# Last chunk of a fused attention-and-GELU kernel: the two token pairs one after the other, and one pair's stores on two queues

## The chip, the cores and the metric

The kernel runs on one core of one Trainium2 chip. The metric is device time in microseconds (us) of one execution, from repeated executions; the profile is one further execution, taken by the hardware profiler. Five engines work side by side, each on its own instruction stream in order: TensorE (PE, with its weight loads shown as PEld), VectorE (DVE), ScalarE (ACT), GpSimd (POOL) and SyncE (SP). ACT and SP also issue transfers (DMAs); such an issue stands in the same stream as the engine's other instructions, and 16 DMA engines then move the data.

## What is computed

The reference, cut to its core (8 batches, 8 heads, sequence 576, head size 64; d_model 512, d_ff 2048):

```python
q_s = softmax(q, axis=-1);  k_s = softmax(k, axis=2)
kv  = einsum('bhsd,bhse->bhde', k_s, v)
att = einsum('bhsd,bhde->bhse', q_s, kv)
x   = att.transpose(0, 2, 1, 3).reshape(B * S, H * D)     # 4608 x 512
h   = x @ w_in                                            # 4608 x 2048
g   = 0.5 * h * (1.0 + erf(h / sqrt(2)))
out = g @ w_out                                           # 4608 x 512
```

All inputs and the output are float32. The kernel multiplies in bf16 and accumulates in float32.

## The kernel before, in words

Tokens are taken in nine chunks of 512: chunks 0 to 7 are the first 512 tokens of each batch, chunk 8 is the eight remainders of 64 tokens. Each chunk has an attention part (`kv_mm`, `x_mm`), a first matrix product with GELU (`h_phase`, `h_pairs` or `h_waves`), and a second matrix product. The order of all instructions is written out by hand: each engine runs its instructions in the order in which the program calls them, and the framework adds only the semaphore waits.

From chunk 1 on, the second product uses a seven-product scheme: the 512 tokens x 512 columns of output are four quadrants c11, c12 (tokens of the first half) and c21, c22 (second half), and instead of eight block products there are seven, `mm(1)` to `mm(7)`, whose left sides are blocks of `g` and sums of them (`s12`, `s5`, made on DVE by `s_parts`) and whose right sides are blocks of `w_out` and sums of them (`w16`, `w7`). Products that are accumulated in the same PSUM bank, and adds on DVE, put the quadrants together.

The last chunk has its own routine, `y_last` (L741 to L811), because nothing follows it that could hide its end. It splits each quadrant once more, into two halves of 128 token columns, j = 0 and j = 1 (the "token pairs"). For each j:

- Each `mm(j, m, ps, first)` (L763) is 8 matmuls of 256 columns into a PSUM bank `ps`; with `first` False it adds to what is in the bank. Product 7 of j = 1 is cut into two of 128 columns in two banks (L807).
- Product 4 goes to bank bd, and ACT copies it to `f`, a part of `zeros32` (L778). Product 5 goes to be, and DVE subtracts it from `f` (L783). Product 1 goes to ba, and DVE adds it to `f` for c22 (j = 0) or c11 (j = 1) (L785). Product 2 is accumulated on bd, and ACT copies the sum to c21 (L789). Product 3 goes to a bank bx (j = 0, copied by ACT at L781) or is accumulated on be (j = 1, copied by ACT at L794), for c12. DVE then completes c22 (L791, L796).
- Product 6 goes to bb and DVE adds it to c22 (L801). Product 7 of j = 0 is accumulated on ba, and DVE writes c11 = `f` + ba (L805); for j = 1 it goes to fresh banks and is added to c11 (L810).
- A quadrant's half is 128 partitions x 256 columns in SBUF, in the tiles `ysb` (`y_sb` in the profile). `store` (L753) sends it out in two DMAs of 64 partitions each (64 KB), u = 0 and u = 1, on the queues that it is given: `sp` is SP's, `act_q` is ACT's.

Before, there are two loops over j. The first makes products 4, (3,) 5, 1, 2 of j = 0 and then 4, 5, 1, 2, 3 of j = 1; the second makes 6 and 7 of j = 0, then 6 and 7 of j = 1. Every DVE add is recorded on the line of the helper `tt`, L428; every matmul of `y_last` on L765; every store on L755. In all there are 16 stores, 11 on SP and 5 on ACT.

Of the kernel before, what the change touches and what calls it, by code (L numbers as in the profile page):

```python
# [16 lines left out]
def kernel(  # L17
# [48 lines left out]
    def bank(i, name="ps", shape=(128, 512)):  # L66
        return psum.tile(list(shape), FP32, tag=f"k{i}", name=name)
# [359 lines left out]
    def tt(out, in0, in1, op=ALU.add, eng=nc.vector):  # L427
        eng.tensor_tensor(out=out, in0=in0, in1=in1, op=op)  # L428
# [232 lines left out]
    def y_operands(c):  # L661
        g = st[c]["g"]
        act = {
            1: s12[:, :, LO], 2: s12[:, :, HI], 3: g[:, UP, LO], 4: g[:, DN, HI],
            5: s5, 6: g[:, UP, HI], 7: g[:, DN, LO],
        }
        wgt = {
            1: w16[:, 0], 2: wo_bf[:, UP, 0:HN], 3: wo_bf[:, UP, HN:DM],
            4: wo_bf[:, DN, 0:HN], 5: wo_bf[:, DN, HN:DM], 6: w16[:, 1], 7: w7,
        }  # L670
        return act, wgt
# [69 lines left out]
    def y_last(c):  # L741

        act, wgt = y_operands(c)
        names = (("x0", "yd"), ("x2", "yx"), ("x1", "ye"), ("ba", "ya"), ("bb", "yb"),
                 ("x3", "yd"), ("kv0", "ye"), ("kv1", "yb"))
        bd, bx, be, ba, bb, bd1, be1, bb1 = (bank(roles[r], n) for r, n in names)
        banks = [(bd, be, bb, ba), (bd1, be1, bb1, None)]
        ysb = [moe_sb.tile([128, 2, DM], FP32, tag="y_sb", name="y_sb", bufs=2) for i in range(2)]  # L750
        dst = out.rearrange("(j u s) n -> u s j n", j=J, u=2)

        def store(half, j, c0, *engs):  # L753
            for u, eng in enumerate(engs):
                eng.dma_start(  # L755
                    out=dst[u, M:S, 2 * half + j, c0:c0 + HN],
                    in_=ysb[half][u * R:(u + 1) * R, j, c0:c0 + HN],
                )

        sp, act_q = nc.sync, nc.scalar  # L760
        halves = [[(bank(roles["x2"], "ya") if ps is None else ps)[:, 0:HN] for ps in banks[j]] for j in range(2)]

        def mm(j, m, ps, first, n=slice(0, HN)):  # L763
            for k in range(HK):
                nc.tensor.matmul(  # L765
                    ps[:, n], act[m][:, k, j * 128:(j + 1) * 128], wgt[m][:, k, n],
                    start=(first and k == 0), stop=(k == HK - 1), skip_group_check=True,
                )

        def parts(j):  # L770
            f = zeros32[:, j * HN:(j + 1) * HN]
            return (f, ysb[0][:, j, 0:HN], ysb[0][:, j, HN:DM], ysb[1][:, j, 0:HN], ysb[1][:, j, HN:DM])

        for j in range(2):
            bd, be, bb, ba = halves[j]
            f, c11, c12, c21, c22 = parts(j)
            mm(j, 4, bd, True)
            nc.scalar.copy(out=f, in_=bd)  # L778
            if j == 0:
                mm(j, 3, bx[:, 0:HN], True)  # L780
                nc.scalar.copy(out=c12, in_=bx[:, 0:HN])  # L781
            mm(j, 5, be, True)
            tt(f, f, be, ALU.subtract)  # L783
            mm(j, 1, ba, True)
            tt(c11 if j else c22, f, ba)  # L785
            if j == 0:
                tt(c12, c12, be)
            mm(j, 2, bd, False)
            nc.scalar.copy(out=c21, in_=bd)  # L789
            store(1, j, 0, sp, sp)  # L790
            tt(c22, c11 if j else c22, c21, ALU.subtract)  # L791
            if j:
                mm(j, 3, be, False)
                nc.scalar.copy(out=c12, in_=be)  # L794
            store(0, j, HN, act_q if j else sp, sp)
            tt(c22, c22, c12)  # L796
        for j in range(2):
            bd, be, bb, ba = halves[j]
            f, c11, c12, c21, c22 = parts(j)
            mm(j, 6, bb, True)  # L800
            tt(c22, c22, bb)  # L801
            store(1, j, HN, act_q, sp)
            if j == 0:
                mm(j, 7, ba, False)
                tt(c11, f, ba)  # L805
            else:
                for r, n in (("x0", slice(0, 128)), ("x1", slice(128, HN))):  # L807
                    ps = bank(roles[r], "ya")
                    mm(j, 7, ps, True, n)
                    tt(c11[:, n], c11[:, n], ps[:, n])  # L810
            store(0, j, 0, act_q, sp)  # L811
# [289 lines left out]
    for c in range(2, B + 1):  # L1101
        nb = c + 2
        if 2 < c and nb < B:
            load(nb)
        elif nb == B:
            load_qrest()
        h_waves(c, q_late if c == 2 else None)
        s_parts(c, 4, 4, (2,))
        yi = {}
        if nb <= B:  # L1110
            yi[8] = [lambda: exp_q(nb)]
            yi[1] = [lambda: norm_q(nb)]
            yi[3] = [lambda: table(AF.Gelu)]
        if nb < B:
            yi[9] = [lambda: exp_k(nb)]
            yi[0] = [lambda: touch_g(c), lambda: cast_v_all(nb)]
        if c < B:
            yi[5] = [lambda: next_x(c, nb)]
            y_phase(c, yi)
        else:  # L1120
            y_last(c)
# [30 lines left out]
```

## Time and profile before

| what | value |
|---|---|
| median of 3 runs | 256.82 us (256.74 to 257.05) |
| the profiled execution's own time | 257.07 us |
| its span | 255.3 us |
| granted TensorE clock over the span | 0.996 |
| PE busy in the last chunk's second product (238.7 to 251.2 us) | 12.42 of 12.50 us |
| last matmul of the program ends | 251.1 us |
| last DVE add | 251.16 to 251.45 us |
| last store: issue starts, issue takes, issue to landing | 252.20 us, 0.68 us, 2.1 us |
| bytes read from and written to HBM | 36.70 MB, 9.44 MB |

The span is what the profiler saw from the first to the last instruction; the execution's own time has 1.8 us around it. A line of a timeline has a start in us from the span's beginning, a duration in us, the engine, the source line, the operation, and out<-in; "x8" means that eight such instructions are merged into one line; in brackets, how long the engine had been idle and what released it. SPq and ACTq are the instruction queues of SP and ACT, on which DMA issues stand: the duration there is that of the issue, not of the transfer. "To landing" is the time from the start of an issue to the arrival of its last part.

### The profile page before, as it was taken

How to read it: one execution, taken by the hardware profiler on the slowest of the kernel's cores; microseconds unless marked ns; L12 is line 12 of the kernel's file. 1: busy time of each engine (PE TensorE's matmuls, PEld its weight loads, DVE VectorE, ACT ScalarE, POOL GpSimd, SP SyncE). 2: the span in 40 equal slices, each digit the busy share in tenths (PEclk: the TensorE clock that was granted, in tenths of full speed). 3: DMA queues.
4: the chain of work that ended last, by engine and by line, in shares of the span. 5: the costliest groups of instructions: out<-in, count | busy, mean ns of one | idle time of the engine just before them, and what ended most of it. 6: DMA issues, size and time to landing. Idle time of an engine off the chain costs nothing.

```text
span 255.3 us, 6533 instructions
## 1 busy us (share of the span) xinstructions
PE 248.8 (97%) x2678; PEld 196.1 (77%) x2678; DVE 208.1 (82%) x365; ACT 188.9 (74%) x320; POOL 67.8 (27%) x65
## 2 busy tenths in 40 slices
PE   7999999999999999999999999999999999999993
PEld 3444445448888888888888888888888888888882
DVE  1878796998986989897889788988898889488962
ACT  4875996699977995899589968896886787148720
POOL 1430034000735067006700580058001800040000
PEclk9999999999999999999999999999999999999998
DMA  7999999994449925980499059904920340022024
GB/s 236 396 389 424 403 406 399 400 410 166 62 143 335 265 65 126 328 336 1 114 299 369 7 95 314 374 3 86 270 63 3 82 164 3 0 87 82 1 54 113
DMA packets 43166, 50.23 MB, mean 197 GB/s; under 512 B 20224, under 2 KB 30464, under 8 KB 42880
## 3 DMA queue, kind: packets, MB, share of 16 engines
q1 hardware_dynamic: 42496, 49.19, 58.0%
q10 hardware_dynamic: 640, 0.62, 1.0%
q8 instruction: 21, 0.34, 0.5%
q14 instruction: 9, 0.07, 0.1%
HBM read 36.70 MB, written 9.44 MB: 181 GB/s over the span
## 4 chain that ended last, share of the span: by engine, by line
PE 93%; DMA 4%; POOL 1%; DVE 0%; issue 0%; SPq 0%
PE qa L497 19%; PE ps L377 11%; PE ya L694 10%; PE qb L497 10%; PE yd L694 10%; PE ye L694 6%; PE ps L637 5%; PE yb L694 5%; PE qc L497 5%; PE yx L694 4%; DMA f<-in_v_dram 2%; PE kv L225 2%; PE ps L343 2%; DMA f<-in_q_dram 2%; PE ya L765 1%; PE yd L765 1%
## 5 line engine op out<-in xcount | busy, mean ns | idle before, releaser
L497 PEld LDWEIGHTS <-quad_s 128*128 128x128 bf16 x448 | 43.8, 98 | 5.3 <-issue 0.2
L694 PEld LDWEIGHTS <-g 128*128 128x128 bf16 x448 | 43.3, 98 | 5.8 <-issue 0.4
L269 POOL TENSOR_TENSOR e<-e,recq 128x2048 bf16<-128x2048 bf16 (+1 forms) x9 | 27.4, 3048 | 72.5 <-DVE recq L264 47.4
L694 PEld LDWEIGHTS <-s 128*128 128x128 bf16 x336 | 32.9, 98 | 3.8
L497 PEld LDWEIGHTS <-wi_bf 128*128 128x128 bf16 x336 | 32.8, 98 | 3.9
L497 PE MATMUL qa<-quad_t,quad_s 128*128 128x256 bf16 x224 | 29.3, 272 | 0.0
L377 PE MATMUL ps<-xT,wi_bf 128*128 128x512 bf16 x128 | 28.1, 379 | 0.0
L428 POOL TENSOR_TENSOR y_sb<-y_sb 128x512 f32<-128x512 f32 x14 | 19.5, 1391 | 24.2 <-DVE y_sb L428 21.3
L263 DVE TENSOR_REDUCE qsum<-e 128x16 f32<-128x1024 bf16 (+1 forms) x12 | 20.9, 1742 | 5.0 <-ACT e L173 5.0
L377 PEld LDWEIGHTS <-wi_bf 128*128 128x128 bf16 x128 | 12.3, 97 | 15.2 <-issue 0.8
L428 DVE TENSOR_TENSOR qb<-qa,r 128x512 f32<-128x512 f32 x28 | 18.1, 693 | 5.8 <-ACT g L521 3.1
L505 ACT COPY qc<-qa 128x512 f32<-128x512 f32 x26 | 13.9, 577 | 12.0 <-PE qa L497 11.5
L383 ACT ACTIVATE g<-ps 128x512 bf16<-128x512 f32 x32 | 17.7, 602 | 6.0 <-PE ps L377 5.7
L521 ACT ACTIVATE g<-r 128x512 bf16<-128x512 f32 x28 | 17.3, 633 | 6.2 <-DVE r L428 6.2
L173 ACT ACTIVATE e<-f 128x512 bf16<-128x512 f32 (+1 forms) x42 | 20.5, 559 | 1.5 <-DMA f<-in_q_dram 1.4
L521 ACT ACTIVATE g<-qc 128x512 bf16<-128x512 f32 x28 | 15.2, 595 | 7.6 <-PE qc L497 7.6
L428 DVE TENSOR_TENSOR r<-qa,r 128x512 f32<-128x512 f32 x28 | 18.0, 685 | 0.9 <-PE qa L497 0.7
L190 POOL CAST v_aug<-f 128x576 bf16<-128x576 f32 x26 | 17.7, 713 | 3.9 <-DMA f<-in_v_dram 3.7
L402 DVE TENSOR_TENSOR s<-g 128x1024 bf16<-128x1024 bf16 x28 | 18.6, 684 | 0.0
L178 ACT ACTIVATE ek<-f 128x2304 bf16<-128x2304 f32 (+1 forms) x10 | 17.4, 1738 | 0.6 <-DMA f<-in_k_dram 0.5
L521 ACT ACTIVATE g<-qb 128x512 bf16<-128x512 f32 x28 | 15.1, 595 | 0.7 <-PE qb L497 0.7
L497 PE MATMUL qb<-quad_t,quad_s 128*128 128x256 bf16 x112 | 15.5, 273 | 0.0
(101 smaller groups left out, 468.7 us busy)
## 6 DMA issues: line engine op xcount, KB each, us to landing
out_dram<-y_sb SPq DMA_DIRECT2D x16, 512.0 KB, 3.4
f<-in_k_dram SPq DMA_DIRECT2D x6, 1152.0 KB, 10.2
f<-in_v_dram SPq DMA_DIRECT2D x6, 1152.0 KB, 11.8
f<-in_q_dram SPq DMA_DIRECT2D x6, 1024.0 KB, 8.2
w<-in_moe_w_in_dram SPq DMA_DIRECT2D x6, 512.0 KB, 8.1
f<-in_v_dram SPq DMA_DIRECT2D x8, 288.0 KB, 6.6
f<-in_q_dram SPq DMA_DIRECT2D x4, 512.0 KB, 9.0
w<-in_moe_w_out_dram SPq DMA_DIRECT2D x2, 1024.0 KB, 11.8
```

Source lines behind the costliest of these rows:

```text
L173: nc.scalar.activation(out=dst[:, i], in_=src[:, u], func=AF.Exp)
L178: nc.scalar.activation(out=ek[b % 2][:, i:i + n], in_=st[b]["kf"][:, i:i + n].rearrange("p x (n d) -> p x n d", n=NS), func=AF.Exp,)
L190: eng.tensor_copy(out=o, in_=i)
L263: nc.vector.reduce_sum(out=qsum, in_=st[b]["eq"][:, :, i * w:(i + 1) * w, :], axis=AX.X)
L269: eng.tensor_tensor(out=e, in0=e, in1=st[b]["recq"].unsqueeze(3).to_broadcast([128, J, w, D]), op=ALU.mult,)
L377: nc.tensor.matmul(ps, wi_bf[:, dm, t * 128:(t + 1) * 128], st[c]["xT"][:, dm, :], start=(dm == 0), stop=(dm == NDM - 1),)
L383: nc.scalar.activation(out=st[c]["g"][:, t, :], in_=ps, func=AF.Gelu)
L402: tt(out=s12[:, a, half], in0=g[:, a, half], in1=g[:, b, hi], op=ALU.add)
L428: eng.tensor_tensor(out=out, in0=in0, in1=in1, op=op)
L497: nc.tensor.matmul(held[kind, q][:, u], w, mov[m][:, k], start=(m in (1, 5) and u == 0 and k == 0), stop=(k == 1), skip_group_check=True,)
L521: nc.scalar.activation(out=g[:, t:t + 2, half], in_=held[kind, q], func=AF.Gelu)
L694: nc.tensor.matmul(ps[:, j * HN:(j + 1) * HN], act[m][:, k, j * 128:(j + 1) * 128], wgt[m][:, k, :], start=(first and k == 0 and j == 0), ...
```

## The change

In `y_last` the second loop over j is gone; its body now stands at the end of the first loop's body. So products 6 and 7 of j = 0, with their two DVE adds and their four stores, come before everything of j = 1. Apart from this one store is changed: the c21 half of j = 1, of which both parts were issued on SP, now has its u = 0 part on ACT. SP issues 10 stores, ACT 6. No other line differs.

```diff
             mm(j, 2, bd, False)
             nc.scalar.copy(out=c21, in_=bd)
-            store(1, j, 0, sp, sp)
+            store(1, j, 0, act_q if j else sp, sp)
             tt(c22, c11 if j else c22, c21, ALU.subtract)
             if j:
                 mm(j, 3, be, False)
                 nc.scalar.copy(out=c12, in_=be)
             store(0, j, HN, act_q if j else sp, sp)
             tt(c22, c22, c12)
-        for j in range(2):
-            bd, be, bb, ba = halves[j]
-            f, c11, c12, c21, c22 = parts(j)
             mm(j, 6, bb, True)
             tt(c22, c22, bb)
             store(1, j, HN, act_q, sp)
```

## The prediction

> **What bounds the kernel now.** I read the page first, for which engine sets the end, then the timeline of the last chunk, then the issues of its last stores one by one. Only the last 17 us can change: no line outside the last chunk's second product differs.
>
> ```profile
> PE 248.8 (97%) x2678; PEld 196.1 (77%) x2678; DVE 208.1 (82%) x365; ACT 188.9 (74%) x320; POOL 67.8 (27%) x65
> PE 93%; DMA 4%; POOL 1%; DVE 0%; issue 0%; SPq 0%
> ```
>
> PE is busy without a break, and the chain that ended last is PE's. So work that PE does is paid in full, order is free as long as PE never waits, and behind PE's last matmul (251.13) there is a tail of adds and stores. In that tail the issues, from windows of the timeline that hold one or two each:
>
> ```profile
> 247.69 1.22 SPq L755 DMA_DIRECT2D out_dram<-y_sb  x1
> 248.97 0.50 ACTq L755 DMA_DIRECT2D out_dram<-y_sb  x1
> 249.00 0.55 SPq L755 DMA_DIRECT2D out_dram<-y_sb  x1
> 249.64 0.76 SPq L755 DMA_DIRECT2D out_dram<-y_sb  x1
> 250.50 0.76 SPq L755 DMA_DIRECT2D out_dram<-y_sb  x1
> 251.16 0.29 DVE L428 TENSOR_TENSOR y_sb<-y_sb,ya 128x128 f32<-128x128 f32 x1 [0.16 <-PE ya L765]
> 251.34 0.77 SPq L755 DMA_DIRECT2D out_dram<-y_sb  x1
> 251.47 0.47 ACTq L755 DMA_DIRECT2D out_dram<-y_sb  x1
> 252.20 0.68 SPq L755 DMA_DIRECT2D out_dram<-y_sb  x1
> ```
>
> The last add ends at 251.45. ACT sends its half of that result 0.02 later, at 251.47; SP sends the other half only at 252.20, because it is still working off older stores: the one at 251.34 is of a result that was ready at 250.68 (DVE's add at 250.26, 0.42 long). That backlog of some 0.7 us began with the issue at 247.69, which took 1.22. The last issue lands 2.1 after its start (2.12 by the trace's stamps), at 254.32, and the span ends 0.97 later. So the span's end hangs on SP's last issue, not on the last add itself.
>
> **The change, part by part.** (1) PE. The 16 matmuls and 16 weight loads of products 6 and 7 of j = 0 move ahead of the 40 of j = 1. Nothing is added: 8 matmuls take 0.87 (243.08 to 243.95 below) in either place. What changes is what PE has to wait for.
>
> ```profile
> 242.38 0.69 DVE L405 TENSOR_TENSOR g<-g 128x1024 bf16<-128x1024 bf16 x1
> 243.08 1.04 PE L765 MATMUL yd<-wo_bf,g 128*128 128x256 bf16 x8
> 243.60 0.42 DVE L428 TENSOR_TENSOR y_sb<-zeros,ya 128x256 f32<-128x256 f32 x1 [0.20 <-DVE zeros L428]
> 243.95 1.04 PE L765 MATMUL ye<-wo_bf,s 128*128 128x256 bf16 x8
> ```
>
> Product 6 takes the slot at 243.08. Its left side was finished by DVE's L404 at 242.46; the first half of its weights much earlier; no wait. Product 7 takes the slot at 243.95. Its left side (L405) is ready at 243.07, but it accumulates on bank ba, which DVE's add for c22 (L785) is reading from 243.60 to 244.02. Before, 4.3 us lay between; now PE must wait. How long after a DVE instruction a waiting matmul starts is seen in an earlier chunk:
>
> ```profile
> 204.45 0.68 DVE L428 TENSOR_TENSOR qb<-qa,r 128x512 f32<-128x512 f32 x1
> 205.19 0.27 PE L497 MATMUL qa<-quad_t,quad_s 128*128 128x256 bf16 x1
> ```
>
> 204.45 + 0.68 = 205.13, so 0.06. Product 7 starts at 244.02 + 0.06 = 244.08, a stall of 0.13; it is on the path that sets the end, and all of j = 1 is 0.13 later. Its bounds: 0.07 (no release time at all) and 0.13 plus 0.33, if the wait also took in the next DVE add, which ends at 244.35. I take 0.13, since the wait is for that one add.
>
> (2) DVE. The same 14 adds. The two moved ones run in what was idle time: DVE waited 0.38, 0.86, 0.45, 0.45 and 0.45 between its adds from 245 on. c22 of j = 0 now follows its predecessor (ends 245.14) by 0.10, as dependent adds do here, and is ready at 245.67; c11 at some 246.0, since product 7 is complete by 245.13.
>
> (3) ACT. Its stream gets two DMA issues, each waiting for DVE, ahead of the copy of `f` for j = 1. Issue of c22 at 245.70, c11 after it; by the rows of ACT, 0.47 to 0.55 each, with 0.05 between, they end at 246.7 to 246.85. Behind them stand, in order: the copy to `f` (0.37 long, its bank ready at 246.0), which ends at some 247.15 instead of 246.4; for this wait DVE's subtraction into `f` and, on PE, product 2 of j = 1, which accumulates on the same bank bd and has its slot at 247.44 + 0.13 = 247.57. Cover: 247.57 less 247.15 and 0.06 is 0.36, so cost nothing. Without that cover each 0.1 us of ACT delay is 0.1 us of the end. Later, the c21 part moved to ACT (0.47 to 0.55, from 249.04) stands ahead of the copy of c12; that makes c12 ready at 249.95, and c22 of j = 1 at 250.93 instead of 250.68 + 0.13. The first half of the last add can then start at 250.85, the second at its old 251.16 + 0.13, because PE's last matmuls come later than that: some 0.15 of cover, cost nothing.
>
> (4) SP. It loses one issue, and its stores come when their results do: two of j = 0 at 246.2 to 247.9 (past the two older ones of c12), then nothing until c21 of j = 1 at 249.04. From there: c21 (0.55 to 0.77), c12 at 249.98, c22 at 250.96, c11. c22's issue by the 0.55 of 249.00 (where ACT began beside it, as it will here) ends at 251.51, and 0.09 lie between two SP issues (249.55 to 249.64), so SP is free at 251.60; by 0.76 it is free at 251.81. The last add ends at 251.45 + 0.13 = 251.58 and releases at 251.60. So SP's last issue starts at 251.60 to 251.81 instead of 252.20. One beside an ACT issue (249.00) landed after 2.2; one alone (252.20) after 2.1. Landing: 251.60 + 2.2 = 253.80 to 251.81 + 2.1 = 253.91. I take 253.85.
>
> **Sum.** 254.32 - 253.85 = 0.47 us less (0.60 of backlog, less 0.13 of stall). The closing 0.97 stays. Span 255.29 - 0.47 = 254.82; own time of that execution 257.07 - 0.47 = 256.60. It ran 0.25 over the median of 256.82, so against the median I say 256.35. 0.2% is 0.51 us here, about what a measurement of this kernel tells from no change; the forecast lies just inside.
>
> One rule speaks against the gain. The Trainium skill (Perfetto Trace Analysis, "DMA Instruction — HWDGE (DVE, Sync)") has a DMA-issuing sequencer lock a shared descriptor generator for itself. By that rule the two issues that one add releases would follow one another. The rows at 248.97 and 249.00 speak against it: 0.50 and 0.55 side by side.
>
> **Rivals.** *Issues of one moment take turns* (the mechanism of that rule). For it: SP's 1.22 at 247.69 and its 0.76 beside ACT's at 250.72, which ended 0.06 after ACT's did. Against: the pair at 249.0. SP's last issue would then pass on 0.47 late and land at 251.60 + 2.2 + 0.47 = 254.27: gain 0.05, 256.77. Chance 0.20.
>
> *ACT becomes the one that is late* (the other sign). If ACT's two early issues run beside SP's and take what SP's worst took, 1.22 each, they end at 248.19, the copy to `f` at 248.61, and product 2 of j = 1 starts at 248.67, a stall of 1.10 on PE. Last add at 252.68, landing at 252.71 + 2.2 = 254.91: 0.59 slower, 257.41. It decides from where the two issues take over 1.8 us together (0.95 + 0.36 of cover + 0.47 of gain). Against: five issues on ACT took 0.47 to 0.55, three of them inside one of SP's. Chance 0.11.
>
> *No stall.* If product 7's first matmul isn't held, because matmuls are written later than the profile shows them start, 0.13 comes back, and with 2.1 to landing the end is 251.47 + 2.1 = 253.57: 256.07 to 256.22. Against: 205.19 above, where PE was held in just this way. Chance 0.16.
>
> *The reorder gives nothing because the tail is the transfers'.* That holds if the last two stores interleave on the DMA engines so that the later lands as now, 2.4 after issue; 251.81 + 2.4 = 254.21, 256.71. Chance 0.03.
>
> **How the numbers follow.** The forecast has 0.50 with 256.25 to 256.45, nearly half of it (0.24) below 256.31. Faster: 0.24 + 0.16 = 0.40. Within 0.2%: 0.26 + 0.20 + 0.03 = 0.49. Slower: 0.11. The range goes from the no-stall case, 256.10, to the turn-taking one, 256.80, and leaves out the late ACT and a few hundredths below.
>
> **What would show it.** Product 7 of j = 0 starting at 244.08, PE without any further gap, its last matmul ending 0.13 later than 251.13; the copy to `f` of j = 1 ending near 247.15; SP's last issue within 0.25 of the last add; last landing near 253.85. A second gap in PE near 247.6 or an ACT issue over 0.8 would make it wrong, and so would a last SP issue that starts in time and lands as late as now.

## The result, and the profile after

| | before | after |
|---|---|---|
| median of 21 runs each | 256.82 us (256.60 to 257.12) | 256.38 us (256.21 to 256.71) |
| span of the profiled execution | 255.3 us | 254.4 us |
| first matmul of the last product, from the span's start | 238.71 us | 238.31 us |
| from there: last DVE add ends | 12.73 us | 12.85 us |
| from there: last landing | 15.62 us | 15.10 us |
| from there: end of the span | 16.58 us | 16.12 us |

The ratio is 0.9982, with a 95% interval of 0.9976 to 0.9988: 0.44 us faster. The spans differ by 0.86 us, but 0.40 of that lies ahead of the last product, where the two programs are the same; such shifts belong to the one execution (over the eleven profiles of this study the last product began at 238.2 to 240.9, the latter in a second profile of the changed kernel). So all times are compared from the first matmul of the last product on, and to hold a time of the changed kernel's timeline against the prediction, 0.40 is added.

The page of the changed kernel, the lines that answer to those of before (busy time of the engines; the chain that ended last):

```profile
PE 248.3 (98%) x2678; PEld 195.9 (77%) x2678; DVE 208.5 (82%) x365; ACT 188.7 (74%) x320; POOL 67.7 (27%) x65
PE 94%; DMA 4%; POOL 1%; ACT 0%; SPq 0%; issue 0%; DVE 0%
```

Nothing is to be seen there, and that is worth knowing: a change of half a microsecond in the tail doesn't show in shares of a 254 us span. The timeline of the last product, changed kernel:

```profile
242.67 1.04 PE L765 MATMUL yb<-w,g 128*128 128x256 bf16 x8
...
243.19 0.42 DVE L428 TENSOR_TENSOR y_sb<-zeros,ya 128x256 f32<-128x256 f32 x1 [0.20 <-DVE zeros L428]
...
243.67 1.03 PE L765 MATMUL ya<-w,g 128*128 128x256 bf16 x8
...
246.72 0.37 ACT L778 COPY zeros<-yd 128x256 f32<-128x256 f32 x1 [3.48 <-PE ye L765]
...
247.16 1.04 PE L765 MATMUL yd<-wo_bf,s 128*128 128x256 bf16 x8
```

Product 6 (yb) starts at 242.67 and keeps its 0.87, so product 7 (ya) had its slot at 243.54; it starts at 243.67, after DVE's add on the same bank ended (243.61); by the trace's stamps 0.05 lie between. That is the stall, 0.12 by the stamps. No view of waits lists it, because a matmul's modelled end (1.04 for 8) runs past the start of the next; the starts give it away, and so does the chain that ended last, where product 7 has 0.99 instead of 0.87. Further down, ACT's copy to `f` ends at 247.09 and product 2 of the second pair, which needs it, starts at 247.16.

The issues of the changed kernel, from narrow windows of its timeline (start, duration of the issue):

```profile
245.30 0.54 ACTq L755 DMA_DIRECT2D out_dram<-y_sb  x1
245.84 0.55 SPq L755 DMA_DIRECT2D out_dram<-y_sb  x1
245.88 0.80 ACTq L755 DMA_DIRECT2D out_dram<-y_sb  x1
...
250.45 0.71 DVE L428 TENSOR_TENSOR y_sb<-y_sb,ya 128x128 f32<-128x128 f32 x2
250.56 0.47 SPq L755 DMA_DIRECT2D out_dram<-y_sb  x1
250.56 0.50 ACTq L755 DMA_DIRECT2D out_dram<-y_sb  x1
251.19 0.48 SPq L755 DMA_DIRECT2D out_dram<-y_sb  x1
251.19 0.75 ACTq L755 DMA_DIRECT2D out_dram<-y_sb  x1
```

And the view of transfers for the last two of these (KB each, us from issue to landing):

```profile
out_dram<-y_sb SPq DMA_DIRECT2D x1, 64.0 KB, 1.9
out_dram<-y_sb ACTq DMA_DIRECT2D x1, 64.0 KB, 2.2
```

The last add ends at 251.16 and both queues send at 251.19. Before, SP was 0.76 late there. The backlog is gone; the later landing is now ACT's, whose issue took 0.75.

### The profile page after: what moved, and what is told of

Same layout as the page of the kernel before. It is cut to its first block, busy times and chain, and to the rows that moved or that the text cites. A ratio compares the mean times of both kernels' runs of the same rounds, so it can differ in the third digit from the quotient of the medians.

```text
span 254.4 us, 6535 instructions
## 1 busy us (share of the span) xinstructions
PE 248.3 (98%) x2678; PEld 195.9 (77%) x2678; DVE 208.5 (82%) x365; ACT 188.7 (74%) x320; POOL 67.7 (27%) x65
## 4 chain that ended last, share of the span: by engine, by line
PE 94%; DMA 4%; POOL 1%; ACT 0%; SPq 0%; issue 0%; DVE 0%
PE qa L497 19%; PE ps L377 11%; PE ya L694 10%; PE qb L497 10%; PE yd L694 10%; PE ye L694 6%; PE ps L637 6%; PE yb L694 5%; PE qc L497 5%; PE yx L694 4%; PE kv L225 2%; DMA f<-in_v_dram 2%; PE ps L343 2%; DMA f<-in_q_dram 2%; PE ya L765 1%; PE yd L765 1%
```

## The experiments

Each kernel ran beside the kernel before on the same chip, and its ratio is to those runs. The experiments ran in three groups (the store alone, the reorder alone, no stall and the first pair on SP; the long stall, the first pair on ACT and the second pair on SP; the last two rows), in which the kernel before had medians of 256.75, 256.75 and 256.84, so medians of different groups compare to about 0.1. The trace columns are from the first matmul of the last product, in us. "Stalls of PE" are by the distances of matmul starts.

| kernel | median, us | ratio to before (95%) | stalls of PE | last add | last landing |
|---|---|---|---|---|---|
| before | 256.82 | | none | 12.73 | 15.62 |
| changed | 256.38 | 0.9982 (0.9976 to 0.9988) | 0.12 | 12.85 | 15.10 |
| the store alone | 256.12 | 0.9977 (0.9968 to 0.9985) | none | 12.74 | 14.97 |
| the reorder alone | 256.35 | 0.9984 (0.9974 to 0.9994) | 0.12 | 12.85 | 15.13 |
| changed, without the stall | 256.26 | 0.9984 (0.9975 to 0.9994) | none | 12.74 | 14.97 |
| first pair's stores on SP | 256.39 | 0.9987 (0.9978 to 0.9997) | 0.12 | 12.85 | 15.14 |
| long stall | 257.19 | 1.0023 (1.0013 to 1.0033) | 0.99 | 13.72 | 15.96 |
| first pair's stores on ACT | 257.62 | 1.0037 (1.0024 to 1.0051) | 0.12, 1.27 | 14.12 | 16.36 |
| second pair's stores on SP | 258.01 | 1.0050 (1.0031 to 1.0069) | 0.12 | 12.86 | 16.96 |
| the store alone, again | 256.20 | 0.9983 (0.9974 to 0.9993) | none | 12.73 | 14.97 |
| changed, again | 256.37 | 0.9984 (0.9975 to 0.9994) | 0.12 | 12.85 | 15.09 |

**The store alone, in the old order.**

```diff
-            store(1, j, 0, sp, sp)
+            store(1, j, 0, act_q if j else sp, sp)
```

> The order of the products as before (two loops), only the c21 part of the second pair moved from SP to ACT. Theory (the gain is SP's backlog, and the reorder only adds a stall of PE of 0.12 us): one issue less on SP clears the backlog in the old order too, SP's last issue starts with ACT's at the last add, the last landing comes 15.0 us after the first matmul of the last product (15.62 before, 15.10 in the changed kernel), PE has no gap; 0.55 to 0.63 us faster than before, so about 256.2 and some 0.13 faster than the changed kernel. Rival (the reorder carries the gain, because the four late stores of the first pair still crowd the end): 0 to 0.15 us faster than before.

Its tail, in the timeline:

```profile
250.49 0.47 SPq L755 DMA_DIRECT2D out_dram<-y_sb  x1
...
250.94 0.29 DVE L428 TENSOR_TENSOR y_sb<-y_sb,ya 128x128 f32<-128x128 f32 x1 [0.16 <-PE ya L765]
...
251.25 0.47 SPq L755 DMA_DIRECT2D out_dram<-y_sb  x1
251.29 0.60 ACTq L755 DMA_DIRECT2D out_dram<-y_sb  x1
```

As the theory had it. One issue less on SP is enough: the issue ahead of the last ends at 250.96, well before the last add does (251.23), and the last one starts 0.03 after that add. The last landing is at 14.97 where 15.0 was said, and 0.13 ahead of the changed kernel's. The rival falls: the late stores of the first pair don't crowd the end once that one issue is off SP.

**The reorder alone**, both parts of c21 back on SP.

```diff
-            store(1, j, 0, act_q if j else sp, sp)
+            store(1, j, 0, sp, sp)
```

> The products in the new order, but both parts of the second pair's c21 on SP as before. Theory: in the new order SP has time for that issue between 248.6 and 249.8, so the backlog is gone without it; as the changed kernel within 0.1 us, about 0.4 us faster than before, PE's gap of 0.12 stays. Rival (the store on ACT carries the gain): 0 to 0.2 us faster than before, or slower by the 0.12 of the gap.

The last add and SP's last issue:

```profile
251.22 0.29 DVE L428 TENSOR_TENSOR y_sb<-y_sb,ya 128x128 f32<-128x128 f32 x1 [0.16 <-PE ya L765]
...
251.64 0.60 SPq L755 DMA_DIRECT2D out_dram<-y_sb  x1
```

Also as the theory had it, 0.03 from the changed kernel's landing, though not quite all of the backlog is gone: SP's last issue starts 0.14 after the last add (0.76 before, 0.03 in the changed kernel). So the two halves of the change don't add up: the store alone clears the whole backlog, the reorder alone most of it, and the second half finds almost nothing left to clear. What they don't share is the stall, which belongs to the reorder.

**The changed kernel without the stall**: product 7 of the first pair goes behind product 4 of the second, its add and stores behind the copy to `f`.

```diff
             mm(j, 4, bd, True)
+            if j:
+                mm(0, 7, halves[0][3], False)
             nc.scalar.copy(out=f, in_=bd)
+            if j:
+                late()
...
             if j == 0:
-                mm(j, 7, ba, False)
-                tt(c11, f, ba)
+                def late(ba=ba, c11=c11, f=f):
+                    tt(c11, f, ba)
+                    store(0, 0, 0, act_q, sp)
...
-            store(0, j, 0, act_q, sp)
+                store(0, j, 0, act_q, sp)
```

> The changed kernel, but the first pair's product 7 is made behind the second pair's product 4, and its add and stores follow ACT's copy to f. Theory (the stall at product 7 is paid in full at the end): PE has no gap in the last product, the last landing comes 0.12 earlier, 0.12 us faster than the changed kernel, about 256.25. Rival (the tail hides the stall, since the end hangs on the queues): the same as the changed kernel within 0.05.

Its timeline around the two products:

```profile
243.91 0.42 DVE L428 TENSOR_TENSOR y_sb<-zeros,ya 128x256 f32<-128x256 f32 x1 [0.20 <-DVE zeros L428]
...
244.27 1.04 PE L765 MATMUL yd<-wo_bf,g 128*128 128x256 bf16 x8
...
245.14 1.04 PE L765 MATMUL ya<-w,g 128*128 128x256 bf16 x8
```

The add still ends at 244.33, but in the slot at 244.27 now stands product 4 (yd), which needs a bank that was never in question, and product 7 (ya) comes 0.87 later. PE has no gap, and the landing is 0.13 earlier. The medians (256.26 to 256.38) agree, but their intervals overlap too much to show 0.12 by themselves; the trace shows it.

**A long stall**: product 7 of the first pair ahead of product 6, to see whether a stall of PE is paid one for one.

```diff
+            if j == 0:
+                mm(j, 7, ba, False)
             mm(j, 6, bb, True)
             tt(c22, c22, bb)
             store(1, j, HN, act_q, sp)
             if j == 0:
-                mm(j, 7, ba, False)
                 tt(c11, f, ba)
```

> The changed kernel with the first pair's product 7 ahead of its product 6, one slot earlier. The bank that it accumulates on is still released only 5.36 us after the first matmul of the last product, and the slot is at 4.37, so PE waits 1.00 instead of 0.12. Theory (a stall of PE here is paid one for one): last matmul, last add and last landing 0.88 later than in the changed kernel, about 257.25. Rival (part of a stall is absorbed by the queues at the end): less than 0.5 us slower than the changed kernel.

```profile
243.08 0.42 DVE L428 TENSOR_TENSOR y_sb<-zeros,ya 128x256 f32<-128x256 f32 x1 [0.20 <-DVE zeros L428]
...
243.56 1.03 PE L765 MATMUL ya<-w,g 128*128 128x256 bf16 x8 [0.83 <-DVE y_sb L428]
```

Now the stall is long enough that the timeline names it: PE idle, released by DVE's add, again 0.05 after its end by the stamps. The view counts 0.83, from the modelled end of the matmul before; by starts PE lost 0.99, 0.87 more than in the changed kernel, and the last add and the landing came 0.87 later. It is paid one for one.

**The first pair's late stores on SP alone**, so that no store stands ahead of ACT's copy to `f`.

```diff
-            store(1, j, HN, act_q, sp)
+            store(1, j, HN, act_q if j else sp, sp)
...
-            store(0, j, 0, act_q, sp)
+            store(0, j, 0, act_q if j else sp, sp)
```

> The changed kernel, but the first pair's c22 and c11 are stored by SP alone, so that ACT's copy to f for the second pair stands behind no store (SP issues 12, ACT 4). Theory (ACT's two early issues have 0.3 us of cover, SP has idle time after them): the copy to f starts some 0.7 us earlier, PE's gap stays at 0.12, the time is that of the changed kernel within 0.1 us. Rival (ACT's delay costs time at the end): faster than the changed kernel by 0.1 us or more. Other rival (SP's extra issues bring the backlog back): slower than the changed kernel by 0.2 us or more.

```profile
245.65 0.37 ACT L778 COPY zeros<-yd 128x256 f32<-128x256 f32 x1 [2.36 <-PE yd L765]
...
247.19 1.04 PE L765 MATMUL yd<-wo_bf,s 128*128 128x256 bf16 x8
```

The copy comes 1.1 us earlier than in the changed kernel (7.30 from the first matmul instead of 8.41; some 0.7 was said), its consumer on PE at the same time (8.85), and the landing 0.04 later. So in the changed kernel the wait on ACT costs nothing, and SP bears the two extra issues there.

**The first pair's late stores on ACT alone**: the same wait made longer.

```diff
-            store(1, j, HN, act_q, sp)
+            store(1, j, HN, act_q, sp if j else act_q)
...
-            store(0, j, 0, act_q, sp)
+            store(0, j, 0, act_q, sp if j else act_q)
```

> The changed kernel, but the first pair's c22 and c11 are stored by ACT alone: four issues instead of two stand ahead of the copy to f for the second pair (SP issues 8, ACT 8). Theory (cover of some 0.3 us, beyond it each 0.1 us of ACT's delay is paid): four issues of 0.5 to 0.8 from 7.0 us after the first matmul of the last product end at 9.3 to 10.3, the copy 0.4 later, product 2 of the second pair starts 0.9 to 1.8 after its slot at 8.85, a second gap of that size in PE, and the kernel is slower than the changed one by the same 0.9 to 1.8 us. Rival (the cover is larger, ACT's stores cost nothing): within 0.2 us of the changed kernel.

```profile
245.40 2.67 ACTq L755 DMA_DIRECT2D out_dram<-y_sb  x4
...
248.11 0.37 ACT L778 COPY zeros<-yd 128x256 f32<-128x256 f32 x1 [4.76 <-DMA out_dram<-y_sb]
...
248.53 1.03 PE L765 MATMUL yd<-wo_bf,s 128*128 128x256 bf16 x8 [1.11 <-ACT zeros L778]
```

The chain reads off line by line: four issues hold ACT until 248.07, the copy ends at 248.48, and product 2 starts 0.05 later, 1.27 after its slot. The landing is 1.26 later than in the changed kernel, the median 1.24. The name in the brackets of the copy (DMA) stands for the store issues ahead of it on ACT, not for their transfers: the copy starts 0.04 after the last issue's end, and that store lands only at 249.52. With no store ahead of it, in the run before this one, the copy was released by PE.

**The second pair's stores on SP alone**, to price an issue in the tail.

```diff
-            store(1, j, 0, act_q if j else sp, sp)
+            store(1, j, 0, sp, sp)
...
-            store(0, j, HN, act_q if j else sp, sp)
+            store(0, j, HN, sp, sp)
...
-            store(1, j, HN, act_q, sp)
+            store(1, j, HN, sp if j else act_q, sp)
...
-            store(0, j, 0, act_q, sp)
+            store(0, j, 0, sp if j else act_q, sp)
```

> The changed kernel, but all eight stores of the second pair are issued by SP (SP 14, ACT 2). Theory (the end hangs on how many issues SP has left at the last add, 0.55 to 0.6 us each with the space between): SP is busy without a break from 10.3 us after the first matmul of the last product, its last issue starts at 14.0 to 14.6 instead of 12.88, the last landing comes 0.9 to 1.6 later than in the changed kernel, 257.3 to 258.0, though PE and the last add are as before. Rival (the transfers themselves set the tail, not the issues): within 0.3 us of the changed kernel.

SP's issues from single windows of its timeline, and in between the last add:

```profile
249.01 0.47 SPq L755 DMA_DIRECT2D out_dram<-y_sb  x1
249.53 0.83 SPq L755 DMA_DIRECT2D out_dram<-y_sb  x1
250.46 0.55 SPq L755 DMA_DIRECT2D out_dram<-y_sb  x1
251.06 0.59 SPq L755 DMA_DIRECT2D out_dram<-y_sb  x1
251.26 0.29 DVE L428 TENSOR_TENSOR y_sb<-y_sb,ya 128x128 f32<-128x128 f32 x1 [0.16 <-PE ya L765]
251.74 0.55 SPq L755 DMA_DIRECT2D out_dram<-y_sb  x1
252.34 0.59 SPq L755 DMA_DIRECT2D out_dram<-y_sb  x1
253.02 0.55 SPq L755 DMA_DIRECT2D out_dram<-y_sb  x1
253.62 0.59 SPq L755 DMA_DIRECT2D out_dram<-y_sb  x1
```

PE and the last add are as in the changed kernel, and yet the landing is 1.87 later and the median 1.63. The theory's direction holds and the rival falls, but the size was over the stated 0.9 to 1.6: eight issues take 0.66 each with the space between ((253.62 - 249.01) / 7), and the last starts 14.9 after the first matmul, not 14.0 to 14.6. The price said had no room for the space, which is 0.05 to 0.09 here.

**The store alone and the changed kernel once more**, side by side on one chip.

> The old order with the one store moved, once more, beside the changed kernel on one chip. Theory: 0.12 us faster than the changed kernel (256.1 to 256.3), the last landing at 14.97 us after the first matmul of the last product, no gap in PE. Rival (the first time was chance): the same as the changed kernel within 0.05.

> The changed kernel itself, for comparison on the same chip. Every theory: 256.3 to 256.45, the last landing at 15.10 us after the first matmul of the last product, one gap of 0.12 in PE.

Both traces came out as the first time (landing at 14.97 and 15.09, a stall of none and 0.12). The medians are 256.20 and 256.37. The version that moves one store and leaves the order alone is ahead of the changed kernel in both comparisons: by 0.19 in the gain over the kernel before (0.63 against 0.44) and by 0.17 in the median side by side, and by 0.13 and 0.12 in the landing. By the median it was the fastest kernel of the study; by the landing the changed kernel without the stall is as early (14.97). The intervals of the ratios overlap, so its lead over the changed kernel rests on the traces.

## Why the prediction held, step by step

- **The end hangs on SP's last issue.** Shown: with the last add 0.12 later than before, the landing came 0.52 earlier; with the last add unchanged and SP loaded, 1.87 later.
- **The stall at product 7**, said 0.13, was 0.12, and the long stall shows that its price is one for one. The rival without a stall is out.
- **DVE's adds in idle time**: c22 of the first pair was ready at 245.26 + 0.40 = 245.66, said 245.67. Nothing on DVE delayed the end.
- **ACT's cover** is the term that was mis-sized. The copy to `f` was to end near 247.15 with 0.36 to spare; it ended at 247.09 + 0.40 = 247.49, since ACT's second issue took 0.80, not the 0.47 to 0.55 of the rows. Product 2 kept its slot (247.16 + 0.40 = 247.56, said 247.57), with 0.01 of the cover left after the release. So the sum came out right, but the rival with the late ACT was much nearer than the prediction's margin: its mechanism is real, as the four stores on ACT show (ACT's last issue ended 1.29 later there than here, and product 2 started 1.27 later), and its price begins right behind where the changed kernel stands. The second issue of the changed kernel, 0.801 by the stamps, also meets the prediction's own sign of being wrong, an ACT issue over 0.8. That ACT cost nothing all the same was luck: 0.35 of the 0.36 of cover were used.
- **SP's last issue** was to start at 251.60 to 251.81; it started at 251.19 + 0.40 = 251.59. That the later landing would be ACT's was not foreseen: the last pair's issues began together, SP's took 0.48, ACT's 0.75. The last landing was at 253.81, said 253.85. It came 2.2 after its issue, so the rival in which the later store lands 2.4 after its issue is out too.
- **The closing time**, said to stay 0.97, was 1.03: with ACT's store landing last, one more of the final waits comes behind it (the waits are taken one after the other, 0.06 apart).
- **Sum**: 0.47 said; 0.52 by landing, 0.46 by the end of the span, 0.44 (0.17%) by the medians, so just inside the 0.2% as forecast. The split in the prediction's bracket (0.60 of backlog less 0.13 of stall) is wrong, though: 252.20 to 251.60 has the stall in it already, so it is taken off twice there; the 0.47 itself rests on the two landings, 254.32 and 253.85. By the traces it is 0.73 of backlog (a last issue 0.76 after the last add before, 0.03 after it now), less 0.12 of stall, less 0.09 because the last landing comes 2.21 after its issue instead of 2.12.
- **Turn-taking.** In three of the last four pairs, where one result released two issues, both ran side by side (0.47 on SP, 0.50 on ACT); in the last pair ACT's took 0.28 longer than SP's, less than the 0.47 of a full turn. The Trainium skill (Perfetto Trace Analysis, "DMA Instruction — HWDGE (DVE, Sync)") has the descriptor generator locked for exclusive use. By that rule the second issue would wait out the first; the issues of those three pairs don't show it. What does show is a shorter delay behind the issue: the first packets of ACT's store began 1.40 to 1.41 after the start of its issue in all four pairs, and 1.13 to 1.20 in ACT's five issues of the kernel before, and it landed after 2.2 instead of 1.9 to 2.0. The forecast's 2.2 was the landing of the second issue of such a pair (249.00), so its price was right and the rival's too high. (Of ACT's five issues before, four and not three stood inside one of SP's.)

What the prediction did not ask is which half of the change pays. It put the whole gain down to SP's backlog, which is right, but the reorder is not needed for it and costs the stall; the moved store alone does it.

What stays open: why an issue beside another takes 0.50 in some pairs and 0.75 to 0.99 in others. Among the last four pairs of the changed kernel, ACT's took 0.75 in the one that began 0.63 after the pair ahead of it, and 0.50 in those that began 0.94 or more after; the repeat, the kernel without the stall and the long stall show the same. But in the store alone a pair 0.99 behind another took 0.98 and 0.99, so nearness by itself is not shown to be the cause.

## What to carry to other kernels

Where a tail is made of stores, list the issues of each queue one by one with the time at which their data was ready: a queue that is late there is worth the lag of its last issue, however busy the compute engine looks, and one issue moved to the other queue may be all that it takes. Before products are reordered, look for the accumulator whose reader stood far away before and is next door now. And when a store goes ahead of compute on an in-order engine, size its cover with the longest issue in the trace, not with the usual one.

## What the hardware showed beyond that

- A matmul held by DVE starts 0.05 after the DVE instruction's end by the stamps (205.19 before, 243.67 after, 243.56 with the long stall); held by ACT's copy, 0.05 (248.53 with the first pair's stores on ACT).
- Of two stores of 64 KB issued 4 ns apart (251.187 on SP, 251.191 on ACT), the packets of the second began 0.29 after those of the first (252.32 and 252.60 by the trace's packets); in the three pairs ahead of it also 0.29. In these four pairs the second store landed 2.2 after its issue, the first 1.9 to 2.0.
- Eight issues in a row on SP cost 0.66 each with the space between, though a single one may show only 0.47.
